# Another order of all steps in a Hedgehog attention and Fourier mixing kernel on one core

## The chip, the core and the metric

The kernel runs on one core of a Trainium2 chip. Its engines are TensorE (PE, with its weight loads shown apart as PEld), VectorE (DVE), ScalarE (ACT), GpSimd (POOL) and SyncE (SP, which here only issues transfers). Each engine executes its own instructions in the order in which the program wrote them, and waits where an operand is not there yet. Transfers are issued by POOL (queue q0) and SP (queue q1) and carried out by 16 DMA engines. The metric is the time of one execution on the device, in microseconds.

## The reference

Eight batches of eight heads with 576 positions and head dimension 64. Linear attention with a feature map of exponentials is followed by a two-dimensional Fourier mix, a normalisation and a feed-forward layer of hidden width 2048:

```python
def phi(x):
    proj = np.einsum('bhsd,df->bhsf', x, w_phi)
    proj = proj - np.max(np.abs(proj), axis=-1, keepdims=True)
    return np.concatenate([np.exp(proj), np.exp(-proj)], axis=-1)
q_p, k_p = (phi(q), phi(k))
kv = np.einsum('bhsf,bhsd->bhfd', k_p, v)
z = np.sum(k_p, axis=2)
num = np.einsum('bhsf,bhfd->bhsd', q_p, kv)
den = np.einsum('bhsf,bhf->bhs', q_p, z)[..., None] + 1e-06
x = (num / den)                      # heads side by side: (8, 576, 512)
X = np.fft.fft(np.fft.fft(x, axis=1), axis=2)
u = x + np.real(X).astype(np.float32)
mu = np.mean(u, axis=-1, keepdims=True)
var = np.mean((u - mu) ** 2, axis=-1, keepdims=True)
un = (u - mu) / np.sqrt(var + 1e-06)
ch = np.maximum(un @ w_ch1, 0.0) @ w_ch2
out = u + ch
```

## The kernel before

The eight batches run through one software pipeline: while PE computes the feed-forward layer of one batch, the attention and the mix of the next are put between its matmuls. Everything is cut into 1238 steps. A step is what a generator issues up to its next yield: a few matmuls on PE and what belongs to them on the other engines. A string PLAN (lines 23 to 37) holds one letter for each step. The kernel walks through it, and each letter calls the next step of its stream; at the end of a batch's steps a stream goes on to the next batch. So PLAN alone sets the order of the instructions on every engine. Nothing else reorders them.

The streams, with the lines that matter:

- F, forward: 16 hidden blocks (matmuls psf, L1224, from the normalised input UT and the first weights W1b; ACT's relu into HT at L1229 and L1231) and the out blocks (pso, L1241, L1267, L1286, from HT and the second weights W2b; DVE adds the residual at L1247, then a store).
- M, mixing: for each head a product of keys and values (kv, L887 and L891; ACT copies it to kvh, L895) and its use by the queries (pn_, L944, L987), then the Fourier mix: pm (L1021), DVE's CEO (L1025, L1034), psD (L1045), ACT's casts to ET and DT (L1050 to L1057), px (L1075), pu (L1104), added to X by DVE (L1089, L1094).
- D, fold: DVE folds X into R (L903 to L927), ACT casts one row to HI (L916, L917), on which pm waits.
- N, normalise: UN (L1139, L1144, L1150) and UT, its transpose, in batch 0 on PE (L1159) and later by a transfer on SP's queue (L1167).
- P, T, R, S: features of keys and queries. The keys' tail of 64 positions is projected at L477 (ps) and its exponentials K4p and K4n are L482 and L483; the main part is projected at L491 (psk) with exponentials KPp and KPn (L497). S scales V by factors from ACT (V4N and V4P at L451, VCn and VCp at L466, with ACT's L447 and L461). In batch 0 that is L852 and L869, with ACT's factors from L862.
- K, V, Q: fetch of the next batches by POOL (L284, into KS, VS, QS); A and B: their transposes by SP (L408 to L422).
- W: two steps. POOL issues the transfer of W1b (L93) and later that of W2b (L95), 2 MB each as they are stored in bf16.
- C and H: constants, and the four sines SS, CS, SD, CD (L238 to L249); POOL's L197 to L218 make their arguments. Z: zeros and ones in padded tiles (L268 to L277). G and J: the first transposes on PE (pst, L368).
- Y: fillers (L1338), four matmuls on ones whose result nobody reads.

Before the first letter, load_first (L336) has SP issue the first batch's K, Q and V, which go into tiles that hold W2b and HT later. V's main part comes in two transfers: heads 0 to 3, then heads 4 to 7. The first batch's heads are taken in pairs, in the order 0, 3, 2, 1, so pair 3 is the first that needs the second half of V.

Of the kernel before, what the change touches and what calls it, by code (L numbers as in the profile page):

```python
# [20 lines left out]


PLAN = (
    "CCZCYYZYGGCTZVTRZKGTGRZWGJTTSJYRSJTQTTPPYTYRPTJMRJTMSMMSPSTKPTPTZMYTMMQTMTPMCQTMMTMTBDMHKMHKHDDHYAHY"
    "DYMYMHYTMMVMRTQMTNMMYTNTQNNYSFNMFNFNRVRFSTTPTFMFRSYUNTFWMURFVFFFFUUMTPMFBSTFMNTUTPNUSMFVPPCTFMFTUPQM"
    "TFMFTFPATVMFFFMMFTFMFKMFFMQFMFRTKFMFFRFPFDFFFFTFFFFTDFFFDRTFFFMFFTTDMFRFFFFSFFMFFFTFMSMFRFTMTTNMTFMN"
    "FPTMMFSSMTPMFTPPMTFFFMFFQNMPTFBSFMFFQMFFPTFFMNNUAMFFMFMFVTRTFFMFFVRVFFKMFKFFFFTMFMFFFFQMFPFDFFTPFRFF"
    "FTFDPFFTFFDDFFRFFTMFFFTMFFMMBSFFMSFRFTMMTFTNNFMFMMMKFTFMTSTFFFFSMPPTMTFFFFFMFSFMFPTMQQVFFFPTKFFMNNNM"
    "FFMFFMFFUMFFMFMFFFAMTRTVFFRTVFFFFFQMFFFDFDFTFFFDRFTPDFFFTPFFRFFTMFFFFTMMMFSFFRSFTMFTFMTTFNFTFMFNSMMM"
    "FMBSFKTTMQNFFFNPFMTFFFMFTPPFMFSFMNFPQMUTFVFKFPAFFMMFMFFVMFFMTFMFFMFFFMRTFRVFFTFFFQMFFFFTDDFRFFFFTFDP"  # L30
    "FFDFTPFFFRFTMTFFFFFMMMFFRFSFSTMSTFFMTFTFFNMFFTNMMMMSTTFMFFQNFTFPMFFFMFVNFMTBPPFSFMFFTPFMKFFFMFFQPNMF"
    "FMAUKFFMFFFMTTFRFRFMFFFTSFFFFVTMFFFRMTQFFFMTFFFFDFDFFFRFDFTFFDMFTFMFFMFSMFMRFTFFTMFTFTFFTMNNFPSMMMMV"
    "TFFSMTPMSTQFFMTPMFTFBQMFPPPFFMFFMFNVFPFFANNUMFFMFMTFMFFMFFMFFRTFRMFFFFFFFVTTPFSFFRFVFFMTFDFFTFFFDFDR"
    "FFFFFTDMTMFFFFFMMFFSFRFTMFTTTMNFMTNMFFFFMSFMMPSTFMFFFNFPTMFFFFFFMTPPSFMFFMFPTFMFFPNFFTMFNMFFMFMFFUFM"
    "FMFFFFMMFFFFFFMFFFFDFFFDFDFFFDFMFFMFFMFFMMFFMNMFFNFFFFFFMFMFMFFFFFFFFFFFFFFFFFFFNFFFFFNFNFFFUFFFFFFF"
    "FFFFFFFFFFFFFFFFFFFFFFFFFFFFFFFFFFFFFF"
)

# [1368 lines left out]
```

## Time and profile before

| | us |
|---|---|
| median of 3 runs | 425.31 |
| lowest and highest | 424.94 and 427.0 |
| span of the profiled execution | 423.1 |
| first hidden matmul of batch 0 (psf) | 53.6 |
| first out matmul of batch 0 (pso) | 85.2 |
| first hidden matmul of batches 2, 3, 4 | 158.2, 205.3, 252.4 |
| end of the last matmul | 418.3 |

The page gives busy time, then the span in forty slices, the DMA queues, the chain of work that ended last, and the costliest groups. The row of the granted TensorE clock (PEclk) has a digit for each slice, 9 being full speed. In a timeline a row gives start and length in us, the engine, the line, what is written from what, and how many instructions are put together (x8); brackets at its end hold the engine's idle time ahead of it and what ended it.

### The profile page before, as it was taken

The page shows a single profiled execution, that of the slowest core. Times are in us where ns is not written, and L with a number is a line of the kernel's source. Part 1 is how long each engine was busy: PE and PEld are TensorE (multiplying, and loading weights), DVE is VectorE, ACT ScalarE, POOL GpSimd, SP SyncE. Part 2 cuts the span into 40 slices and gives each one's busy share as a digit, 9 for nine tenths or more (in the row PEclk, how much of TensorE's full clock was granted, in tenths as well). Part 3 has the DMA queues.
Part 4 walks back from the last instruction along what each step waited for, and adds up shares of the span by engine and source line. Part 5 has one row for each costly group of instructions (what it writes and reads, how often), then busy time and mean ns, then how long its engine had stood idle before and what let it go on. Part 6 is the DMA issues. An engine that isn't in the chain of part 4 may idle for free.

```text
span 423.1 us, 10390 instructions
## 1 busy us (share of the span) xinstructions
PE 397.4 (94%) x4093; PEld 256.1 (61%) x4122; DVE 331.1 (78%) x681; ACT 306.3 (72%) x626; POOL 207.8 (49%) x271
## 2 busy tenths in 40 slices
PE   8787798999899999999999999999999999999995
PEld 3454475744676558655675558665766567656563
DVE  4989788798979976998779885898989786968103
ACT  6978799748975899489847898588868887353460
POOL 7982688525646077706673282834755331500000
PEclk9999999999999999999999999999999999999999
DMA  8999959984569468853899069954895081103313
GB/s 218 206 165 163 148 88 174 145 83 76 89 102 180 72 101 106 123 84 49 112 153 138 2 91 136 131 71 66 117 138 77 14 102 32 27 0 72 72 26 87
DMA packets 108761, 42.70 MB, mean 101 GB/s; under 512 B 82857, under 2 KB 103721, under 8 KB 108713
## 3 DMA queue, kind: packets, MB, share of 16 engines
q0 software_dynamic: 45936, 16.60, 37.1%
q1 hardware_dynamic: 62215, 24.85, 34.8%
q8 instruction: 32, 0.52, 0.5%
q10 hardware_dynamic: 562, 0.59, 0.5%
q14 instruction: 16, 0.13, 0.1%
HBM read 36.77 MB, written 9.44 MB: 109 GB/s over the span
## 4 chain that ended last, share of the span: by engine, by line
PE 61%; DVE 20%; ACT 8%; POOL 5%; DMA 2%; issue 2%; DVEq 0%; ACTq 0%; POOLq 0%
PE psf L1224 21%; PE pso L1241 19%; DVE R L903 3%; PE kv L887 3%; DVE cb L999 3%; DVE tg L994 2%; PE pso L1267 2%; PE psD L1045 2%; DMA UT<-UN 2%; PE pu L1104 2%; PE psq L547 1%; DVE MK L511 1%; PE psk L491 1%; PE psh L597 1%; DVE X L1094 1%
## 5 line engine op out<-in xcount | busy, mean ns | idle before, releaser
L1224 PE MATMUL psf<-UT,W1b 128*128 128x320 bf16 (+1 forms) x1024 | 142.5, 286 | 2.4 <-DMA UT<-UN 1.5
L1241 PE MATMUL pso<-W2b,HT 128*128 128x512 bf16 x467 | 117.1, 379 | 1.7 <-issue 0.5
L1224 PEld LDWEIGHTS <-W1b 128*128 128x128 bf16 x1024 | 94.0, 98 | 29.7 <-issue 4.3
L1229 ACT ACTIVATE HT<-psf 128x320 bf16<-128x320 f32 x128 | 53.5, 442 | 27.0 <-PE psf L1224 21.6
L1241 PEld LDWEIGHTS <-HT 128*128 128x128 bf16 x496 | 44.8, 98 | 44.6 <-issue 2.6
L1002 POOL TENSOR_TENSOR X<-cb,rd 128x320 f32<-128x320 f32 x56 | 41.5, 746 | 38.6 <-DVE rd L1001 37.3
L466 POOL TENSOR_TENSOR VCn<-VS,VCn 128x512 bf16<-128x512 bf16 x28 | 29.7, 1061 | 38.1 <-ACT VCn L461 35.3
L1231 ACT ACTIVATE HT<-psf 128x512 bf16<-128x512 f32 x64 | 37.9, 605 | 12.6 <-PE psf L1224 12.0
L555 DVE TENSOR_REDUCE MQ<-psq 128x8 f32<-128x1024 f32 (+1 forms) x32 | 34.3, 1084 | 13.4 <-PE psq L547 13.2
L1247 DVE SCALAR_TENSOR_TENSOR X<-pso,rs,X 128x512 f32<-128x512 f32 x31 | 22.8, 735 | 21.6 <-PE pso L1241 21.6
L497 ACT ACTIVATE KPn<-psk 128x1024 bf16<-128x1024 f32 x28 | 28.6, 1021 | 14.0 <-DVE MK L511 13.9
L497 ACT ACTIVATE KPp<-psk 128x1024 bf16<-128x1024 f32 x28 | 28.7, 1025 | 11.1 <-PE psk L491 11.1
L451 POOL TENSOR_TENSOR V4N<-VS,V4N 64x256 bf16<-64x256 bf16 x14 | 8.7, 623 | 53.9 <-ACT V4N L447 53.4
L511 DVE TENSOR_REDUCE MK<-psk 128x8 f32<-128x1024 f32 x28 | 33.9, 1212 | 1.0 <-ACT KPp L497 0.7
L1094 DVE TENSOR_TENSOR X<-pu,X 128x512 f32<-128x512 f32 (+3 forms) x49 | 23.3, 526 | 11.2 <-PE pu L1104 8.9
L466 POOL TENSOR_TENSOR VCp<-VS,VCp 128x512 bf16<-128x512 bf16 x28 | 29.7, 1059 | 0.0
L606 ACT ACTIVATE QPHP<-psh 128x1024 bf16<-128x1024 f32 x28 | 28.9, 1031 | 0.8 <-PE psh L597 0.6
L606 ACT ACTIVATE QPHN<-psh 128x1024 bf16<-128x1024 f32 x28 | 29.0, 1035 | 0.0
L1150 ACT ACTIVATE UN<-X,MV 128x512 bf16<-128x512 f32 (+1 forms) x35 | 24.5, 723 | 5.4 <-DVE MV L1175 3.1
L1174 DVE BATCH_NORM_STATS2 st<-X 128x6 f32<-128x512 f32 (+1 forms) x40 | 27.1, 677 | 0.3
L1190 POOL TENSOR_TENSOR rs<-VE,mhalf 128x5 f32<-128x5 f32 (+1 forms) x9 | 10.3, 1145 | 29.0 <-DVE VE L1189 29.0
L987 PEld LDWEIGHTS <-QPHP 128*128 128x128 bf16 x280 | 21.2, 99 | 4.6 <-DVE cb L999 1.0
(465 smaller groups left out, 825.0 us busy)
## 6 DMA issues: line engine op xcount, KB each, us to landing
out_dram<-X SPq DMA_DIRECT2D x15, 256.0 KB
out_dram<-X SPq DMA_DIRECT2D x60, 64.0 KB
QS<-in_q_dram POOLq DMA_DIRECT2D x14, 256.0 KB, 6.2
KS<-in_k_dram POOLq DMA_DIRECT2D x7, 512.0 KB, 7.4
VS<-in_v_dram POOLq DMA_DIRECT2D x14, 256.0 KB, 5.1
W1b<-in_moe_w_ch_dram POOLq DMA_DIRECT2D x1, 2048.0 KB, 13.1
W2b<-in_moe_w_ch_dram POOLq DMA_DIRECT2D x1, 2048.0 KB, 14.8
W2b<-in_k_dram SPq DMA_DIRECT2D x2, 512.0 KB
```

What stands on the lines that cost most here:

```text
L466: nc.gpsimd.tensor_tensor(out=VC[:, hs, :, 0:D], in0=values[b][0][:, hs, :].rearrange("p h (j d) -> p h j d", d=D), in1=VC[:, hs, :, D:D + ...
L497: nc.scalar.activation(out=KP[:, hs, :, :].rearrange("p e (jp jj) f -> p jj (e jp) f", jj=2), in_=psk[:], func=AT.Exp, scale=sgn,)
L511: nc.vector.tensor_reduce(out=MK[:, 2 * pr:2 * pr + 2, :].rearrange("p e (jp jj) -> p jj (e jp)", jj=2), in_=tiles[pr][:], axis=AX.X, op=A ...
L555: nc.vector.tensor_reduce(out=o, in_=i[:], axis=AX.X, op=ALU.max, apply_absolute_value=True)
L606: nc.scalar.activation(out=o, in_=psh[:], func=AT.Exp, scale=sgn)
L1002: nc.gpsimd.tensor_tensor(out=X[:, :, D * h:D * h + D], in0=cb[:, :, 0:D], in1=rd[:].to_broadcast([128, 5, D]), op=ALU.mult,)
L1094: nc.vector.tensor_tensor(out=to, in0=more, in1=to, op=ALU.add)
L1174: nc.vector.bn_stats(out=st[0:M, :], in_=X[0:M, c, 0:C])
L1224: nc.tensor.matmul(ps, lhsT=W1b[:, cc, 128 * hh:128 * hh + 128], rhs=UT[:, cc, lo:hi], start=(cc == 0), stop=(cc == NCC - 1),)
L1229: nc.scalar.activation(out=HT[:, hh, lo:hi], in_=ps, func=AT.Relu, scale=-1.0)
L1231: nc.scalar.activation(out=HT[:, hh - 1:hh + 1, lo:hi], in_=psw[:].rearrange("p (a n) -> p a n", a=2), func=AT.Relu, scale=-1.0,)
L1241: nc.tensor.matmul(po[:], lhsT=HT[:, hh, at:at + 128], rhs=W2b[:, hh, :], start=(hh == 0), stop=(hh == NHH - 1),)
```

## The change

Only the string PLAN is replaced. The number of steps and of each letter are the same; all fourteen lines of it differ. Its first line before and after:

```diff
 PLAN = (
-    "CCZCYYZYGGCTZVTRZKGTGRZWGJTTSJYRSJTQTTPPYTYRPTJMRJTMSMMSPSTKPTPTZMYTMMQTMTPMCQTMMTMTBDMHKMHKHDDHYAHY"
+    "ZYZCYYCCGCGTWGRTGZTTJZYRPYTSJTJRSPTGJSTRPTKJTMMYMRSSTMPKTPTQPTBMTMZQMMTTPMCQZMMTTMVDTHHYMHAMYDHDDYYY"
```

POOL in the first 17 us, before the change. QPHP, QPHN, V4P, V4N and HI are padded tiles that are filled once; gs, gc and ga are arguments of the sines; VS and KS are parts of batch 1's values and keys:

```order
L197 TENSOR_SCALAR gs<-ga,pn 128x320 x3
L268 MEMSET QPHP 128x8x64
L268 MEMSET QPHN 128x8x64
L212 TENSOR_SCALAR gc<-gc,pn 128x512
L215 TENSOR_SCALAR gc<-gc 128x512
L218 TENSOR_TENSOR ga<-ga,gc 128x512
L271 MEMSET V4P 128x520
L284 DMA VS_249<-in_v_dram 64x4x64 x2
L271 MEMSET V4N 128x520
L284 DMA KS_265<-in_k_dram 64x8x64
L274 MEMSET HI_105 128x512
L93 DMA W1b<-in_moe_w_ch_dram 128x4x2048
```

(between the last two there is a second memset of the same kind, for HI's other tile). POOL at the same place in the changed program:

```order
L268 MEMSET QPHP 128x8x64
L268 MEMSET QPHN 128x8x64
L197 TENSOR_SCALAR gs<-ga,pn 128x320 x3
L212 TENSOR_SCALAR gc<-gc,pn 128x512
L215 TENSOR_SCALAR gc<-gc 128x512
L218 TENSOR_TENSOR ga<-ga,gc 128x512
L93 DMA W1b<-in_moe_w_ch_dram 128x4x2048
L271 MEMSET V4P 128x520
L271 MEMSET V4N 128x520
L852 TENSOR_TENSOR V4N<-HT,V4N 64x4x64 x2
L852 TENSOR_TENSOR V4P<-HT,V4P 64x4x64 x2
L869 TENSOR_TENSOR VCn<-HT,VCn 128x8x64
```

W1b's transfer moved ahead of the V4 memsets; the transfers of VS and KS and the HI memsets moved behind the scaling of the first V; the two L268 memsets moved ahead of L197.

ACT around the fold of batch 0, before the change (HI is the row that pm waits for; ps and psk are projected keys of batch 1, ET and DT results of the mix):

```order
L247 ACTIVATE SD<-ga 128x512
L916 CAST HI_105<-R 1x257
L917 CAST HI_105<-R 1x255
L249 ACTIVATE CD<-ga,halfpi 128x512
L482 ACT_TABLE_LOAD
L482 ACTIVATE K4p<-ps_880 128x512
L483 ACTIVATE K4n<-ps_880 128x512
L1053 CAST ET<-psD 128x289
L1054 CAST ET<-psD 128x289
L1057 ACTIVATE ET<-psD 128x2x31
```

And in the changed program:

```order
L247 ACTIVATE SD<-ga 128x512
L249 ACTIVATE CD<-ga,halfpi 128x512
L916 CAST HI_105<-R 1x257
L917 CAST HI_105<-R 1x255
L482 ACT_TABLE_LOAD
L482 ACTIVATE K4p<-ps_861 128x512
L483 ACTIVATE K4n<-ps_861 128x512
L497 ACTIVATE KPp<-psk 128x2x4x128
L497 ACTIVATE KPn<-psk 128x2x4x128
L1053 CAST ET<-psD 128x289
L1054 CAST ET<-psD 128x289
L1057 ACTIVATE ET<-psD 128x2x31
```

The last sine (CD) moved ahead of the HI casts, and the first exponentials of KPp and KPn of batch 1 ahead of the ET casts. On PE the projection for K4p (L477) stands directly ahead of pm (L1021) in the changed program, and behind pm and eight fillers before; the projection for that first KPp (L491) stands between pm and the first psD (L1045), and before the change behind all of psD and px.

Behind the first out matmul the letters of all streams are dealt anew as well. On PE, runs of matmuls of the same shape are longer there: 136 changes between array shapes (which rows and columns of the array a matmul uses) in place of 151.

More of the change, by code (lines that the diff above doesn't have):

```diff
@@ L23 @@
 PLAN = (
-    "CCZCYYZYGGCTZVTRZKGTGRZWGJTTSJYRSJTQTTPPYTYRPTJMRJTMSMMSPSTKPTPTZMYTMMQTMTPMCQTMMTMTBDMHKMHKHDDHYAHY"
[L25 to L33, printed above, removed]
@@ L34 @@
-    "FFFFFTDMTMFFFFFMMFFSFRFTMFTTTMNFMTNMFFFFMSFMMPSTFMFFFNFPTMFFFFFFMTPPSFMFFMFPTFMFFPNFFTMFNMFFMFMFFUFM"
-    "FMFFFFMMFFFFFFMFFFFDFFFDFDFFFDFMFFMFFMFFMMFFMNMFFNFFFFFFMFMFMFFFFFFFFFFFFFFFFFFFNFFFFFNFNFFFUFFFFFFF"
+    "ZYZCYYCCGCGTWGRTGZTTJZYRPYTSJTJRSPTGJSTRPTKJTMMYMRSSTMPKTPTQPTBMTMZQMMTTPMCQZMMTTMVDTHHYMHAMYDHDDYYY"
+    "HTMTMTMHRYVMRSMQTVKTQPMNMYTYNRNTMTSNUNYTFMMFRFNFNUFFSFMKNRUFMFNPSFWMTTPMFCFFTNBFFPFUMPTFSMTFMPTFMTUF"
+    "TUPQTFMUFFATMFMFMFFMFMFMFMKFTRFFRFTFFFFFDDQDTVPQFVFFDVTFFFMTFTFFMFFRRFFFFSVFFKSFMMFTFFFFTSMRFFSMTMTN"
@@ new lines @@
+    "FFNPMMBTFMMTPSFPMTMTPMFTFFMTPFMFFQFMFPFTFFMNNNMFMFFVMFMFFMVFFMFMFATTFRURFTMKFFFFFFFTTPFFDFFFRDFFQKFF"
+    "FPTQFFFDFFRFDFTMFFFTTSFMMMFFFFRBFMSFPTMFTNFSSFMNMFFFMMMTTTFFVFPFFSMTPMTFFFMQFFNMFNFFMPTFAMFFPTFMNMFV"
+    "FMFFMMUFFMFFMFFFMFFTMFFFDTRTTFFQKFFRDFFVFTFFFDRPFFFDSFFTPFFRFFMFFFTQTTFFMMFFFSMRFMFTSTTMFFFNTFMFNMMM"
+    "FFMTTMFFFNKPMSTNSPFMFFFTNPQMFFFFUMFBVTFPMFFMFPMMVFFFMAFMFFFTTMFRFSFTMFFFFMFRFDKFFTFFTFMQFRFFFFFDFSDK"
+    "PPFDSFFTFFFFRTMFFFTVFTMFFMMQFRFFPSMFTTTMMSNFNFMMFFMMFFBPFMTTFFFFMVQTPMFVFMFTFMFNFFMPTFKMTFAFFFPFMFTN"
@@ L36 @@
+    "TFMFNUFFTFRMFFRFFMFFFSFFFMFFMFFFMTFFFDTMRFDFFFTFFFQFDVDFFFQFRMFTTMTFFFMSMFRFFMFTTTQMFKMFMTNNSMFMFMFT"
+    "SPFFMFFTPMFFTMTPMTFFFNMPSBFFFPPFVMFFMFFAPNNMUFFMMFFFMFFMFFMFTTFFRMFFFFTSRFFFTPTFFFMFRFFDDFFTFFFFRFFF"
+    "DDFVFTVTMFFMFTFFMFFMFRSFMFTTSTMMFFNNFTMSFMNMMFFFFTPFFFMTPMFPTSFFMNFFFMFFPPMFFMFTPTFFFMNFUMFFMFMFFMFF"
+    "MFFFMMFFFMFFFFFDFFDFFFFDFFDFFMFFFFMMMFFMFFFMFNFFMNFFFMNFMFFFNFMFFFFFFFFFFFFFFNFFFFUFFFFFFFFFFFFFFFFF"
     "FFFFFFFFFFFFFFFFFFFFFFFFFFFFFFFFFFFFFF"
```

## Prediction

> **What bounds the kernel now.** I read the page first, for which engine is full and at what clock, then the windows of the stages, then the chain of waits and the timelines of the stages that are not full.
>
> ```profile
> span 423.1 us, 10390 instructions
> PE 397.4 (94%) x4093; PEld 256.1 (61%) x4122; DVE 331.1 (78%) x681; ACT 306.3 (72%) x626; POOL 207.8 (49%) x271
> PEclk9999999999999999999999999999999999999999
> 0.00:45.90 45.90, 36.31 (x423) 21.35 (x423) 37.53 (x83) 35.01 (x64) 33.88 (x60) 1.00 1.06 184
> 45.90:78.00 32.10, 27.44 (x347) 19.64 (x347) 24.12 (x61) 31.02 (x67) 22.60 (x28) 1.00 1.09 142
> 78.00:418.30 340.30, 333.64 (x3326) 215.06 (x3354) 268.98 (x538) 240.31 (x496) 151.29 (x184) 1.00 0.66 86
> L1224 PE MATMUL psf<-UT,W1b 128*128 128x320 bf16 (+1 forms) x1024 | 142.5, 286 | 2.4 <-DMA UT<-UN 1.5
> ```
>
> A window's row gives start, end and length, then busy time on PE, weight loads, DVE, ACT and POOL, the granted clock and the DMA share. From 78 on PE is busy 333.64 of 340.30 us: that stage only becomes shorter if PE has less to do or waits less for UT. Of the first 45.9 us PE is busy 36.31, part of it fillers, so others set that pace; from 45.9 to 78 ACT does (31.02 of 32.10). What the head gains or loses is passed on whole, since PE's backlog behind it is full. The profiled span is 423.1 us and the median of the three runs 425.31: what lies around the span is 2.2 us, which I add to every sum.
>
> **The head: the weight load.** POOL is in the chain of waits here.
>
> ```profile
> 8.86 2.52 SPq L336 DMA_DIRECT2D HT<-in_v_dram  x4
> 10.44 1.27 POOL L218 TENSOR_TENSOR ga<-ga,gc 128x512 f32<-128x512 f32 x1
> 14.78 1.01 POOL L274 MEMSET HI<- 128x512 bf16 x2
> 15.71 0.79 POOL L93 DMA_DIRECT2D W1b<-in_moe_w_ch_dram  x1
> 19.31 1.06 POOL L869 TENSOR_TENSOR VCn<-HT,VCn 128x512 bf16<-128x512 f32 x1
> 23.30 1.06 POOL L869 TENSOR_TENSOR VCp<-HT,VCp 128x512 bf16<-128x512 f32 x1
> 25.76 1.06 POOL L869 TENSOR_TENSOR VCn<-HT,VCn 128x512 bf16<-128x512 f32 x1 [1.40 <-ACT VCn L862]
> ```
>
> W1b is issued at 15.71, and the chain runs over POOL's scaling of V (L852, L869) until about 24.4, where pair 3 is done. In the new order W1b stands directly behind L218. Two V4 memsets, the VS and KS transfers and the HI memsets no longer come before it, so it is issued at about 11.7 (L218's end) instead, 4.0 us earlier. The transfers of V, which SP issued up to 11.4, are then still running. What that does is read from the queues.
>
> ```profile
> q1 hardware_dynamic: 553, 0.55, 107.8%
> ...
> q1 hardware_dynamic: 241, 0.23, 33.5%
> ...
> q0 software_dynamic: 193, 0.79, 97.1%
> q1 hardware_dynamic: 192, 0.05, 9.3%
> ...
> W1b<-in_moe_w_ch_dram POOLq DMA_DIRECT2D x1, 2048.0 KB, 13.1
> ```
>
> The first row is 13.0 to 14.5: V alone in SP's queue q1, 553 packets of 1 KB, 369 a us, 23 a us on each of the 16 DMA engines. The second is 14.5 to 16.5: the last 241, which at that pace are through at about 15.2. The third and fourth are 22 to 26, where W1b in POOL's queue q0 meets transposes in q1: 193 packets against 192. The engines alternate one for one, and a packet of W1b (4 KB) costs 16 x 4.0 x 0.971 / 193 = 0.322 us. W1b has 2 MB / 4 KB = 512 packets, 32 an engine, together 10.3 us.
>
> Its first packet comes some 1.5 us after the issue (13.1 from issue to landing, less 10.3, with part of the rest at the end): about 13.2. V then has about 241 + 553 x 1.3/1.5 = 720 packets left, 45 an engine. That is more than 32, so all of W1b passes in between and V ends 10.3 us later, at 25.5; with 1.0 for the landing 26.5. The two scalings of pair 3 (the second half of V) end 2 x 1.06 later, at 28.6, where they ended at 24.4. Behind that point the new order is faster: the 1.40 us that POOL waits for L862 (which stands on ACT behind kvh evictions) falls by some 0.85, as three evictions are ahead of it and not four. So the fold starts **3.4 us later**. Bounds: V through before W1b's first packet, -2.5 (two transfer issues and three memsets no longer stand before L852); a first packet with all of V still to go, +4.5.
>
> Row 193:192 first: the Trainium skill, "DMA: Bandwidth & Descriptors", section "Queues, rings and completion order", says that an engine goes round the queues in whole packets of about 9 to 17 descriptors each. If V's groups held 16 rows and W1b's 8, an estimate by that page, 45 rows of V would let only three groups, 24 rows of W1b, 7.7 us, pass; V would land at 23.9 and the sum below be 2.6 us lower, 422.3. The trace shows equal numbers, so I keep one for one; no run here shows these two transfers together.
>
> **The clock.** PE has nothing else ready while it waits for pair 3: what stands before it in the new order is what before ended at 23.1 (and a projection, 0.4), so about 5 us idle.
>
> ```profile
> 22.94 0.19 PE L891 MATMUL kv<-V4N,K4n 128*128 128x65 bf16 x1
> 24.42 0.29 PE L887 MATMUL kv<-VCp,KPp 128*128 128x65 bf16 x4 [1.28 <-POOL VCp L869]
> ...
> 418.30:422.50 4.20, 0.00 (x0) 0.00 (x0) 0.48 (x1) 0.00 (x0) 0.00 (x0) 1.00 0.26 74
> 422.60:423.10 0.50, 0.00 (x0) 0.00 (x0) 0.00 (x0) 0.00 (x0) 0.00 (x0) 0.50 0.00 0
> ...
> 1.11 5.45 PE L1338 MATMUL idle<-ones_b 128*128 128x512 bf16 x12 [1.11 <-DVE keep L130]
> 36.73 3.18 PE L1338 MATMUL idle<-ones_b 128*128 128x512 bf16 x12
> ```
>
> After the last matmul the clock stays 1.00 for 4.2 us and then is 0.50. Twelve fillers at the start took 5.45 us, at full clock 3.18: one spell of half clock costs 2.3. An idle time of 5 us passes 4.2 by less than it is uncertain, so I take 0.4 of that, **+0.9**; bounds 0 and 2.3, or more in a rival below. The Trainium skill, "TensorE: Matmul & The Clock Gate", section "Part 1: The HAM clock gate", gives a free-running window of 3.4 us, one idle window halving the clock; 5 us would hold a whole one in about (5 - 3.4)/3.4, half of the cases, an estimate that gives +1.1 in place of 0.9. The trace's 4.2 lies between one window and two, so it agrees.
>
> **After the fold.** ACT waits twice.
>
> ```profile
> 40.96 0.41 ACT L916 CAST HI<-R 1x257 bf16<-1x257 f32 x1 [1.44 <-DVE R L912]
> 41.58 0.72 ACT L249 ACTIVATE CD<-ga,halfpi 128x512 bf16<-128x512 f32 x1
> 44.59 1.28 ACT L482 ACT_TABLE_LOAD   x1 [2.29 <-PE ps L477]
> 46.85 0.41 ACT L1053 CAST ET<-psD 128x289 bf16<-128x289 f32 x1
> 41.94 2.10 PE L1338 MATMUL idle<-ones_b 128*128 128x512 bf16 x8
> 44.10 0.41 PE L477 MATMUL ps<-wphi,KT 64*64 64x128 bf16 x8
> ```
>
> The table load for L482 waits 2.29 us for keys that stand on PE behind pm and eight fillers. In the new order they are projected before pm, and the last sine (CD) runs ahead of HI, in the 1.44 us wait. So 2.29 + 0.72 = 3.0 us leave ACT's path, and ACT has two key exponentials done before ET. DVE's CEO still comes at its old distance from the fold, which I put at 0.5: **-2.5**, bounds 0 and -3.0. As ACT is the bound to 78, this is passed on.
>
> **Steady state.** Counted from the new order, PE changes between its array shapes 136 times after the first out matmul, and 151 times before the change.
>
> ```profile
> 92.18 1.46 PE L1241 MATMUL pso<-W2b,HT 128*128 128x512 bf16 x6
> 93.47 0.38 PE L1021 MATMUL pm<-HI,ones_b 128*128 128x512 bf16 x1
> 93.90 0.81 PE L1241 MATMUL pso<-W2b,HT 128*128 128x512 bf16 x3
> 94.65 0.40 PE L491 MATMUL psk<-wphi,KT 64*128 64x128 bf16 x8
> ```
>
> Six pso of one shape take 93.47 - 92.18 = 1.29, 0.215 each; three from 93.90 would end at 94.55, and the 64-row psk starts at 94.65. A change costs 0.10, so fifteen fewer give **-1.5** (bounds 0 and -3.0). The eight more changes ahead of it (62 for 54) lie where PE is not the bound.
>
> ```profile
> 205.29 1.47 PE L1224 MATMUL psf<-UT,W1b 128*128 128x256 bf16 x12 [1.00 <-DMA UT<-UN]
> 252.41 1.48 PE L1224 MATMUL psf<-UT,W1b 128*128 128x256 bf16 x12 [0.47 <-DMA UT<-UN]
> ```
>
> PE waits for UT 1.00 us at batch 3 and 0.47 at batch 4. Between mixing's last step and the first hidden matmul the new order has 8.00 and 7.82 us of PE work, for 7.59 and 7.49: **-0.7**, bounds 0 and -1.5. Other moved steps (keys, queries, fetches) fill the same PE time with the same rows; their rings of PSUM buffers are about as tight, so I put them at 0, with 1.5 to both sides. W2b's load goes out three steps of F later; its landing after 14.8 us still leaves 3 us to the first out matmul.
>
> **Sum.** 3.4 - 2.5 + 0.9 - 1.5 - 0.7 = -0.4: a span of 422.7, a time of **424.9 us**, no change that can be measured. A measurement here can tell about 0.5%, 2.1 us, from none.
>
> **Rivals.**
> 1. V is through before W1b comes (the software queue starts later than 1.5 us; POOL's two L268 memsets now stand ahead of L197, and may push L218). Then 3.4 becomes -2.5 and the clock costs nothing: 424.9 - 5.9 - 0.9 = 418.1. For it: a small transfer that POOL issued at 12 into the full queues took 3.9 us, most of it waiting. Against it: even that comes before V is through. 0.2.
>
> ```profile
> VS<-in_v_dram POOLq DMA_DIRECT2D x2, 32.0 KB, 3.9
> ```
>
> 2. Slower: the wait for pair 3 passes the gate by a wide margin, and the clock stays half until the fold, because the work of the heads comes in small pieces with waits between. From 28.37 to 34.69 the chain is nearly all PE, 6.3 us, which at half clock is 6.3 more and not 0.9: 430.3. It decides from 4.2 us idle on. For it: an idle time of 5. Against it: that passes 4.2 by less than the error of the landing time, and steps of several heads lie ready behind pair 3.
>
> ```profile
> 28.37 0.86 PE idle L1338 x4
> ...
> 34.36 0.33 PE pn__730 L944 x10
> ```
>
> 0.2.
> 3. The order does not keep its steady gain: new waits for PSUM buffers (keys for the next batch stand closer to M's steps) take 1.5 and the 2.2 of both steady terms do not come: 424.9 + 3.7 = 428.6. For it: 6.7 us of PE idle from 78 on are few, so any new wait shows. 0.15.
>
> **How the numbers follow.** Forecast 0.45, rival 1 0.2, rival 2 0.2, rival 3 0.15. Half a per cent puts the bounds at 423.2 and 427.4. The forecast's own range is 422 to 428, by the bounds of its terms: 0.3 of it within, 0.1 below (the middle price of the steady terms is not their greatest), 0.05 above. Rival 1 is faster, rival 2 slower; of rival 3 0.1 stays within, where only part of the gain is lost, and 0.05 is slower. So faster 0.1 + 0.2 = 0.3, same 0.3 + 0.1 = 0.4, slower 0.05 + 0.2 + 0.05 = 0.3. The range, 418.0 to 429.8, leaves out half of rival 1 and half of rival 2, 0.2 in all.
>
> **What would show it.** W1b issued near 11.7 and pair 3's VCp ending near 28.6 (right), or by 23 (rival 1); PEclk below 1.00 in windows from 28 to 36 (rival 2); ACT's table load at L482 with no wait; the first psf of batches 3 and 4 with waits under 0.7 us; PE idle from the first out matmul on falling by about 2 us. I am wrong if the fold starts earlier than before, or if the stage behind 85 us changes by more than 4.

## The result, and the profile after

The changed kernel takes 433.0 us, median of four runs (432.95, 433.1, 431.56 and 441.57), the kernel before 425.1. The ratio is 1.016, 95% interval 1.0128 to 1.0192: **slower by 1.6%**, where I had forecast 424.9 and a range up to 429.8. The run of 441.57 lies 2% above the others and is left out of the ratio, as such runs are from the ratios below.

The page of the changed kernel, the same lines as before the change:

```profile
span 431.1 us, 10416 instructions
PE 405.1 (94%) x4122; PEld 258.1 (60%) x4122; DVE 332.6 (77%) x681; ACT 307.3 (71%) x626; POOL 207.9 (48%) x271
PEclk9899999999999999999899998999999999999999
L1224 PE MATMUL psf<-UT,W1b 128*128 128x320 bf16 (+1 forms) x1024 | 144.4, 289 | 7.8 <-DMA UT<-UN 7.3
```

PE looks as busy as before (94%), but that share hides the loss: the clock row now has an 8 in three slices, and the wait of the first layer for UT rose from 1.5 to 7.3 us. (Of PE's larger busy time, 7.7 us, about half is a matter of records: 29 pso are missing in the trace of before and none here, and pso's busy time is 121.0 us for 117.1.)

Where the 8 us arise is seen from windows cut at the same events in both traces: the first HI cast, the first hidden matmul of batch 0, the first out matmul, then the first hidden matmul of batches 2, 3, 4 and 5 (the table goes on to the end of the last matmul). First the changed kernel:

```profile
0.00:38.80 38.80, 34.68 (x404) 20.50 (x404) 30.66 (x73) 32.21 (x61) 30.83 (x57) 0.96 1.03 189
38.80:52.20 13.40, 10.10 (x98) 5.38 (x98) 12.96 (x31) 12.49 (x25) 7.90 (x12) 1.00 0.89 123
52.20:80.80 28.60, 27.62 (x367) 20.76 (x366) 23.10 (x59) 25.60 (x57) 18.65 (x21) 1.00 1.07 132
80.80:154.20 73.40, 71.32 (x695) 42.32 (x693) 65.31 (x125) 55.40 (x111) 43.94 (x55) 1.00 0.94 119
154.20:205.10 50.90, 46.67 (x498) 29.88 (x495) 43.51 (x85) 39.03 (x81) 26.08 (x32) 1.00 0.70 90
205.10:258.90 53.80, 48.73 (x498) 30.63 (x498) 41.83 (x75) 35.44 (x72) 28.51 (x36) 0.97 0.74 93
258.90:308.20 49.30, 48.16 (x494) 31.28 (x494) 37.48 (x75) 38.63 (x79) 24.15 (x29) 0.97 0.62 89
```

And two of the same stages before the change:

```profile
158.20:205.30 47.10, 45.38 (x469) 29.29 (x474) 40.18 (x82) 38.36 (x79) 26.02 (x32) 1.00 0.66 90
205.30:252.40 47.10, 46.14 (x486) 30.10 (x490) 38.19 (x77) 35.74 (x74) 27.00 (x34) 1.00 0.92 101
```

| stage | before | after | difference |
|---|---|---|---|
| start to the first HI cast | 41.0 | 38.8 | -2.2 |
| to the first hidden matmul | 12.6 | 13.4 | +0.8 |
| to the first out matmul | 31.6 | 28.6 | -3.0 |
| to batch 2 | 73.0 | 73.4 | +0.4 |
| batch 2 to batch 3 | 47.1 | 50.9 | +3.8 |
| batch 3 to batch 4 | 47.1 | 53.8 | +6.7 |
| batch 4 to batch 5 | 48.1 | 49.3 | +1.2 |
| batch 5 to the last matmul | 117.8 | 118.1 | +0.3 |

So the head, where I expected the fold to be late, is 4.4 us faster up to the first out matmul, and three stages in the middle lose 11.7. PE's waits there, from the timeline of the changed kernel:

```profile
205.05 2.49 PE L1224 MATMUL psf<-UT,W1b 128*128 128x256 bf16 x12 [3.81 <-DMA UT<-UN]
242.11 1.01 PE L1045 MATMUL psD<-SS,CEO 128*128 128x289 bf16 x6 [1.65 <-ACT HT L1229]
258.93 1.05 PE L1224 MATMUL psf<-UT,W1b 128*128 128x256 bf16 x8 [2.58 <-DMA UT<-UN]
```

Two of them are followed by half clock, in windows laid over it:

```profile
205.40:208.70 3.30, 3.30 (x26) 1.94 (x24) 0.15 (x1) 1.17 (x2) 0.98 (x2) 0.50 0.47 58
259.95:263.30 3.35, 3.35 (x33) 2.67 (x30) 0.00 (x0) 2.77 (x6) 0.41 (x1) 0.50 0.71 134
```

Each such spell is 3.4 us at half speed and costs PE 1.7 us of work. In the stage from batch 3 to 4 there are one spell (1.7), the wait at psD (1.65, and 0.42 at the next one) and 2.1 us more for UT: 5.9 of the 6.7. The bracket at psD names ACT's HT. ACT was late there itself, held by DVE's L511 (from ACT's timeline):

```profile
240.72 1.02 ACT L497 ACTIVATE KPn<-psk 128x1024 bf16<-128x1024 f32 x1 [3.13 <-DVE MK L511]
```

That L511, at 239.47, stands on DVE behind the fold, which the second place below explains.

Two places explain the waits. **The first is a fetch in the way of the transposes.** POOL's issue ahead of batch 3's first hidden matmul in the changed kernel, from its timeline:

```profile
194.25 0.93 POOL L284 DMA_DIRECT2D KS<-in_k_dram  x1
```

SP's, from the same:

```profile
196.92 2.67 SPq L1167 DMA_TRANSPOSE UT<-UN  x2
```

The DMA queues of the changed kernel for 3.6 us from that issue on (packets, MB, share of 16 engines):

```profile
q0 software_dynamic: 981, 0.49, 107.8%
q1 hardware_dynamic: 323, 0.23, 20.8%
```

The queues of the kernel before, for 3.6 us from its own UT issue at 199.9 on (a K transpose that SP issued at 202.57 is among them):

```profile
q1 hardware_dynamic: 1136, 0.37, 78.9%
```

Both kernels store the same rows of X ahead of UT and transpose the same UT. Now 981 packets of batch 5's K fetch fill the engines, and q1 (stores, then UT) moves 323 packets in 3.6 us where it moved 1136. The small packets of the transposes begin 3.3 us after the issue of UT (at 200.2) and not 1.2 us (at 201.1). One for one, as the prediction read it off W1b, does not describe these two queues: 981 stand against 323, and why is open. In the chain of the changed kernel the piece "UT<-UN" is 6.62 us long:

```profile
198.29 6.62 DMA UT<-UN
```

Before the change it was 3.90:

```profile
201.25 3.90 DMA UT<-UN
```

**The second is DVE behind POOL.** Batch 4's fold in the changed kernel, from DVE's timeline:

```profile
235.26 4.02 DVE L920 TENSOR_TENSOR R<-R 128x510 f32<-128x510 f32 x2
```

POOL's at the same time:

```profile
235.09 0.94 POOL L284 DMA_DIRECT2D KS<-in_k_dram  x1
236.04 1.07 POOL L466 TENSOR_TENSOR VCn<-VS,VCn 128x512 bf16<-128x512 bf16 x1
237.06 1.06 POOL L466 TENSOR_TENSOR VCp<-VS,VCp 128x512 bf16<-128x512 bf16 x1
```

The same DVE line before the change:

```profile
232.71 1.27 DVE L920 TENSOR_TENSOR R<-R 128x510 f32<-128x510 f32 x2
```

Two L920 take 1.27 us together before the change and 4.02 here; the first of them is 3.4 us long, and ends 0.6 us behind POOL's second L466, about the length that it needs by itself (0.68). In the order of before POOL had nothing to do at that place. This is so far a coincidence in time; x3_scale_later below tests it.

### The profile page after: what moved, and what is told of

It reads as the page before. It is cut to its first block, busy times and chain, and to the rows that moved or that the text cites. A ratio compares the mean times of both kernels' runs of the same rounds, so it can differ in the third digit from the quotient of the medians.

```text
span 431.1 us, 10416 instructions
## 1 busy us (share of the span) xinstructions
PE 405.1 (94%) x4122; PEld 258.1 (60%) x4122; DVE 332.6 (77%) x681; ACT 307.3 (71%) x626; POOL 207.9 (48%) x271
## 4 chain that ended last, share of the span: by engine, by line
PE 52%; DVE 23%; ACT 16%; DMA 4%; issue 3%; POOL 1%; DVEq 0%; ACTq 0%; POOLq 0%
PE psf L1224 20%; PE pso L1241 14%; DMA UT<-UN 4%; DVE cb L999 4%; DVE tg L994 3%; DVE X L1094 3%; PE kv L887 2%; PE psD L1045 2%; ACT QPHN L606 2%; PE pso L1267 2%; DVE MK L511 2%; ACT QPHP L606 2%; DVE st L1174 2%; DVE R L920 1%; ACT KPp L497 1%
## 5 line engine op out<-in xcount | busy, mean ns | idle before, releaser
L1224 PE MATMUL psf<-UT,W1b 128*128 128x320 bf16 (+1 forms) x1024 | 144.4, 289 | 7.8 <-DMA UT<-UN 7.3
L1241 PE MATMUL pso<-W2b,HT 128*128 128x512 bf16 x496 | 121.0, 379 | 0.0
L1224 PEld LDWEIGHTS <-W1b 128*128 128x128 bf16 x1024 | 95.9, 99 | 36.9 <-issue 6.8
L466 POOL TENSOR_TENSOR VCn<-VS,VCn 128x512 bf16<-128x512 bf16 x28 | 29.6, 1057 | 43.4 <-ACT VCn L461 34.6
L511 DVE TENSOR_REDUCE MK<-psk 128x8 f32<-128x1024 f32 x28 | 33.8, 1209 | 0.0
L497 ACT ACTIVATE KPp<-psk 128x1024 bf16<-128x1024 f32 x28 | 28.6, 1021 | 5.6 <-PE psk L491 5.5
L466 POOL TENSOR_TENSOR VCp<-VS,VCp 128x512 bf16<-128x512 bf16 x28 | 29.5, 1055 | 0.0
L284 POOL DMA_DIRECT2D QS<-in_q_dram x28 | 23.4, 836 | 1.1 <-DMA QT<-QS 1.1
```

What stands on the lines that cost most here:

```text
L466: nc.gpsimd.tensor_tensor(out=VC[:, hs, :, 0:D], in0=values[b][0][:, hs, :].rearrange("p h (j d) -> p h j d", d=D), in1=VC[:, hs, :, D:D + ...
L497: nc.scalar.activation(out=KP[:, hs, :, :].rearrange("p e (jp jj) f -> p jj (e jp) f", jj=2), in_=psk[:], func=AT.Exp, scale=sgn,)
L511: nc.vector.tensor_reduce(out=MK[:, 2 * pr:2 * pr + 2, :].rearrange("p e (jp jj) -> p jj (e jp)", jj=2), in_=tiles[pr][:], axis=AX.X, op=A ...
L1224: nc.tensor.matmul(ps, lhsT=W1b[:, cc, 128 * hh:128 * hh + 128], rhs=UT[:, cc, lo:hi], start=(cc == 0), stop=(cc == NCC - 1),)
L1241: nc.tensor.matmul(po[:], lhsT=HT[:, hh, at:at + 128], rhs=W2b[:, hh, :], start=(hh == 0), stop=(hh == NHH - 1),)
```

## Experiments

All kernels differ from one of the two only in PLAN. A step is written as letter, batch and number (K5.1 is the second K fetch of batch 5).

### Head against rest

The first two exchange the parts at step 320, about the first hidden matmul of batch 1.

```diff
 h1_new_head
-PLAN before
+first 320 steps of PLAN after, then all others in the order of PLAN before
 h2_new_rest
-PLAN after
+first 320 steps of PLAN before, then all others in the order of PLAN after
```

> The first 320 steps of the new order (up to the first hidden matmuls of batch 1), then all that is left in the order of before. In the trace of the change the head is 4.4 us shorter at the first out matmul (80.8 for 85.2) and 4.1 us at the first hidden matmul of batch 2 (154.2 for 158.2); everything is lost between there and 260 us. If head and rest are independent: 425.1 - 4.2 = 420.9 us, between 420 and 422. If the early head merely moves a wait (the steady part is bound by something that does not start earlier, such as transfers), the gain melts away: 424 to 426.

Measured: 420.8 us, ratio to before 0.986 (0.9819 to 0.9897). First out matmul at 81.2, and the stages behind it as before the change (47.1 us from batch 2 to batch 3).

> The mirror of it: the first 320 steps as before, then what is left in the new order. If the loss belongs to the new order of the steady part alone: 433.0 + 4.2 = 437.2 us, 435 to 439. If the loss comes from transfers that arrive at an unlucky moment because the head is early, it goes with the old head: 425 to 429.

Measured: 438.7, ratio 1.029 (1.0259 to 1.0322), with a UT wait of 4.03 at batch 3. Head and rest add up: the head brings 5.3 to 5.7 us (426.2, the kernel before in that comparison, less 420.8; 438.7 less 433.0), the rest of the new order costs some 12. The new head on the old rest beats both kernels.

### The fetch

```diff
 x1_k5_early (PLAN after)
-K5.0 F2.30 ... F2.66 N3.2 K5.1 P4.2
+K5.0 K5.1 F2.30 ... F2.66 N3.2 P4.2
```

> The changed kernel with one step moved: the second K fetch of batch 5 (512 KB, issued by POOL at 194.3 us, three us ahead of batch 3's UT transposes) stands directly behind the first K fetch of that batch, some 30 us earlier. Theory A (the fetch's packets in q0 slow the stores and the UT transposes in q1, so that UT lands late and PE idles 3.8 us at 205.05, after which the clock is 0.66 for 5 us): the wait at batch 3 falls to under 1.2 us, the clock there stays 1.00, and the time falls by 3.8 - 0.5 + 1.7 = 5.0 to about 428 (427 to 429.5). Theory B (UT is late because its inputs are late: the order of the mixing steps, DVE and ACT): the fetch does not matter, 432 to 434, with the wait at batch 3 still over 3 us.

Measured: 428.5 (ratio to before 1.0037, 1.0006 to 1.0068), 4.5 less than the change by the medians of two comparisons, in which the kernel before took 425.1 and 426.2; by the ratios it is 5.2. The wait and the slow clock at batch 3 are gone, as PE's timeline shows; psD and UT of batch 4 wait as they did (1.65 and 2.40):

```profile
204.06 1.47 PE L1224 MATMUL psf<-UT,W1b 128*128 128x256 bf16 x12 [0.34 <-DMA UT<-UN]
```

The window behind it has full clock:

```profile
205.00:210.00 5.00, 5.00 (x77) 3.98 (x75) 3.35 (x7) 4.74 (x11) 5.00 (x7) 1.00 0.92 146
```

The mirror of it puts the collision into the kernel before:

```diff
 b1_k5_late (PLAN before)
-T3.17 K5.1 F2.11 ... R4.4 S4.1 F2.55
+T3.17 F2.11 ... R4.4 S4.1 K5.1 F2.55
```

> The kernel of before with one step moved: the second K fetch of batch 5 (512 KB) goes from some 30 us before the UT transposes of batch 3 to 2 to 3 us before them (between two scalings of V on POOL, at about 197.5), the place that the change gave it. Theory A: the wait for UT at batch 3, 1.0 us before, grows to 3.5 to 4.5 and the clock falls to 0.5 for a window of 3.4 us behind it: 425.5 + 3 + 1.7 = 430 (428.5 to 431). Theory B (the fetch is harmless, the new order of the other steps makes UT late): 425 to 426.5.

Measured: 429.3, ratio 1.0088 (1.0065 to 1.0111). One fetch moved costs 3.8 us (429.3 less 425.5, the kernel before in that comparison). The wait in PE's timeline:

```profile
206.77 2.51 PE L1224 MATMUL psf<-UT,W1b 128*128 128x256 bf16 x11 [2.73 <-DMA UT<-UN]
```

Slow clock follows here too, in the window:

```profile
205.00:210.00 5.00, 3.23 (x24) 2.51 (x25) 1.12 (x2) 1.04 (x2) 2.36 (x3) 0.66 0.75 145
```

The next kernel was to clear the transposes of batches 4 and 5 as well.

```diff
 x2_all_fetches (as x1_k5_early, and)
-F3.61 F3.62 B6.0 ... M5.2 V6.0 Q6.2 ... F4.0 V6.1 F4.1
+F4.4 B6.0 ... F4.5 V6.0 Q6.2 ... F4.7 V6.1
-K7.0 ... Q7.2 M5.21 F4.57 K7.1
+K7.0 K7.1 ... F5.1 Q7.2
```

> The same, and the transfers around the UT transposes of batches 4 and 5 moved as well: batch 6's K transposes and its V and last Q fetches behind batch 4's first hidden matmuls, batch 7's second K fetch directly behind its first, its last Q fetch behind batch 5's first hidden matmuls. Theory A: the UT waits at batch 4 (2.6) and batch 5 (0.9) and the slow clock behind them (1.7 each) go as well, except for what a late fold leaves at batch 4 (one DVE instruction of L920 takes 3.4 us there in place of 0.7): 433 - 5 - 1.1 - 3.4 = 423.5, between 421 and 426. Theory B: 432 to 434. If L920's long instruction is a chance of that one execution, batch 4's wait goes entirely and the time is at the lower end.

Measured: 427.2 (ratio 1.0015, 0.9986 to 1.0044), a miss by 3 to 4 us. Batch 5's wait (0.92 in the changed kernel) is gone, but batch 4's has grown to 4.2, and PE's clock is 0.50 from 255 to 260. POOL's timeline tells why the edit did nothing there: the V fetches that I had put behind batch 4's first hidden matmuls were issued as early as ever, from 245.03 to 248.55.

```profile
245.03 1.28 POOL L284 DMA_DIRECT2D VS<-in_v_dram  x2
```

And PE's wait:

```profile
255.74 0.61 PE L1224 MATMUL psf<-UT,W1b 128*128 128x256 bf16 x2 [4.20 <-DMA UT<-UN]
```

A place in the program is a time only on an engine that is kept waiting there. POOL had no instruction with a wait between the old place and the new one, so it ran ahead.

### POOL beside DVE's fold

```diff
 x3_scale_later (as x1_k5_early, and)
-F3.39 S5.1 D4.2 K6.1 P5.0 P5.1 F3.40 D4.3 S5.2 ... R5.3 T5.6 M4.16
+F3.39 D4.2 K6.1 P5.0 P5.1 F3.40 D4.3 ... R5.3 T5.6 M4.16 S5.1 S5.2
```

> The changed kernel with batch 5's second K fetch early (as in x1_k5_early) and one thing more: the first two scalings of batch 5's V (POOL L466, four instructions, with ACT's factors) stand behind the first psD step of batch 4's mix and no longer on both sides of batch 4's fold (DVE L920). In five traces of the new order that one L920 takes 3.41 us in place of 0.68, from 235.26 to 238.68, while POOL issues a K fetch and runs L466 twice up to 238.12; in the order of before, where POOL waits at that place, it takes 0.68. Theory A (POOL's work holds DVE's access up until it pauses): L920 back to 0.7 us, the wait at psD (1.65) gone, UT 2.7 us earlier, the wait at batch 4 (2.4) down to about 1.3 and the slow clock behind it (1.7) gone: 428.5 - 1.65 - 1.1 - 1.7 = 424 (423 to 426). Theory B (L920 is slow there for another reason, its operands or PSUM): L920 stays at 3.4 us and the time within 1 us of 428.5.

Measured: 424.7 (ratio 0.9982, 0.9956 to 1.0008). L920 is back to 1.27 for two, batch 4's wait for UT down to 0.46, and no half clock follows. But POOL's L466 now runs beside the next DVE steps, CEO (L1034, L1070), and these become long instead, so that psD still waits 1.71. DVE's timeline of x3_scale_later:

```profile
230.31 1.27 DVE L920 TENSOR_TENSOR R<-R 128x510 f32<-128x510 f32 x2
235.47 2.02 DVE L1034 TENSOR_TENSOR CEO<-R 128x381 bf16<-128x381 f32 x2
237.41 1.02 DVE L1070 CAST CEO<-R 128x6 bf16<-128x6 f32 x1
```

POOL's L466 is longer there too: 1.36, from 235.71, for 1.06 elsewhere. PE's wait:

```profile
239.60 0.91 PE L1045 MATMUL psD<-CS,CEO 128*128 128x289 bf16 x6 [1.71 <-DVE MK L511]
```

Elsewhere two L1034 take 1.03 us, L1070 0.17. The total came out as expected, its parts did not: the wait for UT fell by 1.9 (2.40 to 0.46) where I had put 1.1, and the waits at psD by 0.4 (1.65 and 0.42 to 1.71) where I had put 1.65.

That POOL's work holds L920 is shown by this run, but not which part of it: the K fetch's issue, K6.1, went out earlier as well, at 226.69, since POOL had nothing to wait for ahead of it. Another fetch's issue speaks for the scalings: in the changed kernel POOL issues QS from 230.72 to 231.65, and DVE's L903 beside it (from 230.99), which also has two inputs in SBUF, takes its usual 1.28 for two.

```diff
 x4_v6_later (as x3_scale_later, and)
-M5.2 V6.0 Q6.2 ... F4.0 V6.1 F4.1 ... F4.7 K7.0
+M5.2 Q6.2 ... F4.0 F4.1 ... F4.7 K7.0 V6.0 V6.1
```

> As x3_scale_later, with the two V fetch steps of batch 6 (VS, POOL issues at about 245 to 249, beside the UT transposes of batch 4) put behind the K fetch step that follows, which waits on POOL until the K transposes are through, at about 258; so they really go out later. (In x2_all_fetches the same steps were moved on paper only: nothing that waits stood between, and POOL issued them at 245.0 to 248.6 all the same.) If fetches that run beside them slow the UT transposes, the wait at batch 4 falls to under 0.5 us and the time to 1 us below x3: 422 to 424. If not, the time is that of x3.

Measured: 426.2 (423.07 to 431.99; ratio 1.0012, 0.998 to 1.0043). The fetches do go out later, at 261.7, but the time does not fall: nothing is shown on these two, and in the profiled execution V's second half came late in the head, as the next part tells.

### W1b and the first loads

My forecast rested on W1b meeting V. In the changed kernel it hardly did: POOL issued W1b at 11.16, but the queue has none of its packets up to 15. The queues from 13 to 15:

```profile
q1 hardware_dynamic: 714, 0.71, 104.7%
```

And from 15 to 16:

```profile
q0 software_dynamic: 32, 0.13, 65.1%
q1 hardware_dynamic: 210, 0.20, 57.4%
```

So 4 us pass from issue to first packet, not 1.5, and V is nearly through. To see whether the alternation itself is real, W1b was issued at 3.1:

```diff
 w1_first (PLAN after)
-Z0.0 Y0.0 Z0.1 ... T0.0 W0.0 G0.2
+W0.0 Z0.0 Y0.0 Z0.1 ... T0.0 G0.2
```

> The changed kernel with the W1b step first of all, so that POOL issues the 2 MB ahead of its L268 memsets, at about 4 us in place of 11.2, while SP's K, Q and V loads are all in the queue. My forecast said that W1b's packets alternate with V's one for one from 1.5 us after the issue; in the trace of the change W1b was issued at 11.16 but its first packet came at about 15.2, when V was nearly through, and V was not late. If packets alternate as soon as the descriptors are there: W1b's first packets at 6 to 8 us, V lands some 8 us later, at about 24, and the time rises by 5 to 8, to 438 to 441. If a transfer of POOL's gets going only when the other queue is nearly empty: first packet still at 14 to 15, time 432 to 434.

Measured: 444.0, ratio 1.042 (1.0367 to 1.0467). W1b's first packets come from 7.4 on, 4.3 us after the issue, while q1 is full, so they do not wait until the other queue has emptied. The queues from 7 to 8:

```profile
q1 hardware_dynamic: 503, 0.28, 104.1%
q0 software_dynamic: 9, 0.04, 18.1%
```

From 12 to 16 us the queues go one for one:

```profile
q0 software_dynamic: 189, 0.77, 95.1%
q1 hardware_dynamic: 189, 0.10, 11.7%
```

And POOL waits ten microseconds for V, in its timeline:

```profile
22.88 1.31 POOL L852 TENSOR_TENSOR V4N<-HT,V4N 64x256 bf16<-64x256 f32 x2 [10.01 <-DMA HT<-in_v_dram]
```

That W1b takes turns with the first loads and makes V late is as I had it, with a price above my estimate (11 us for 5 to 8); the moment was wrong, by some 2.5 us. In the profiled execution of x4_v6_later, whose head is the changed kernel's, V's second half is late. POOL's timeline there:

```profile
25.39 1.06 POOL L869 TENSOR_TENSOR VCn<-HT,VCn 128x512 bf16<-128x512 f32 x1 [6.11 <-DMA HT<-in_v_dram]
```

And its queues from 18 to 24 us:

```profile
q0 software_dynamic: 304, 1.25, 102.8%
q1 hardware_dynamic: 40, 0.04, 2.4%
```

V's last packets pass at 6.7 a us where V alone makes 357. One engine that alternates with W1b (0.33 us a packet) passes 3 a us, so it is what two or three of the sixteen engines would make, on which W1b would have begun too soon; that is an estimate, no view shows the engines one by one. The first out matmul comes at 88.4, 7.6 us later than in the changed kernel's own profile. A kernel with W1b safely behind V:

```diff
 h3_w_later (as h1_new_head, and)
-T0.0 W0.0 G0.2 ... P0.0 Y0.4 T0.4 S0.0 J0.1
+T0.0 G0.2 ... P0.0 Y0.4 T0.4 S0.0 W0.0 J0.1
```

> As h1_new_head (new head, old rest), with W1b's issue moved behind the scaling of V's tail (POOL L852), to about 17 us, where V's 2 MB are through on every DMA engine. In one trace of the new head (x4_v6_later) some engines began W1b before V's last packets, V's second half came at 25.4 in place of before 19, and the first out matmul was 7.3 us later; in the five other traces it did not happen. If that is the cause of the scatter upwards of kernels with the new head (441.6 once among 432 to 433, 436.4 once among 425 to 431): median as h1, 420 to 422 (W1b lands at 30 and is first used at 52), and no execution more than 2 us above it. If the scatter has another cause, it stays.

Measured: 421.7 (420.83 to 422.36), ratio 0.9898 (0.9879 to 0.9918). W1b is issued at 16.98 and the time is that of h1_new_head within its interval: W1b's early issue is not what makes the new head fast. Six runs lie within 1.6 us; that the scatter of the others comes from W1b alone is likely, not shown.

### Where the head's gain comes from

Three kernels take parts of the new head into the kernel before.

```diff
 b2_fold_part (PLAN before)
-H0.2 D0.1 D0.2 H0.3 Y0.7 A1.0 H0.4 Y0.8 D0.3 Y0.9 M0.14 Y0.10 M0.15 H0.5 Y0.11 T1.0 M0.16 ... T1.1
+H0.2 A1.0 Y0.7 D0.1 H0.3 D0.2 D0.3 Y0.8 Y0.9 Y0.10 H0.4 T1.0 M0.14 T1.1 M0.15 M0.16 H0.5 ...
 b3_pool_part (PLAN before)
-V1.0 ... K1.0 ... Z0.4 W0.0 ... S0.0 ... K1.1
+S0.0 W0.0 ... K1.0 K1.1 V1.0 Z0.4
 b4_pool_and_fold: both
```

> The kernel of before, with only the 23 steps around batch 0's fold in the order that the change gave them (keys for K4 ahead of pm, the last sine ahead of HI, the first KPp ahead of ET). My forecast's term for this part was -2.5 us, bounds 0 and -3.0. If it is right and passed on whole: 425.3 - 2.5 = 422.8 (422 to 423.5). If the gain at the fold is taken back before the first out matmul (ACT stays full to 78 us and does the same work), 425.

Measured: 425.6, ratio 0.9995 (0.9979 to 1.0011). ACT's wait ahead of the table load is gone, but ACT now waits for psD instead, in its timeline:

```profile
41.69 1.28 ACT L482 ACT_TABLE_LOAD   x1
47.47 0.40 ACT L1050 CAST DT<-psD 128x289 bf16<-128x289 f32 x1 [1.76 <-PE psD L1045]
```

The first out matmul, at 84.9, is 0.3 us earlier than before the change.

> The kernel of before, with only the head of POOL's order changed: the first VS and KS transfers, the HI memsets and W1b's issue stand behind the scaling of V's tail (L852) or of all of V (L869) and no longer ahead. In the trace of the change L852 starts at 14.33 in place of 16.51 and the first HI cast at 38.77 in place of 40.96. If this is where the head's first half comes from: HI at about 38.8 and the time 425.5 - 2.2 = 423.3 (422.7 to 424). If the gain is lost again before the first out matmul: 425 to 426.

Measured: 425.3, ratio 1.0003 (0.9984 to 1.0022). POOL's L852 starts at 14.65, 1.9 us earlier, but the first HI cast only 0.24 earlier, at 40.72: POOL's first L869 is 1.0 earlier and not 1.9, since W1b is issued in between, it waits the same 1.40 us for ACT's factors of L862, and DVE's conversion L220, which took 0.42, now runs beside POOL's HI memset (L274) and takes 1.55.

> The same, with the 23 steps around the fold in the new order as well, as in b2_fold_part (which alone took nothing off: 425.6). If POOL's part alone carries: 423.3. If the two together make the head's whole 4.4 us: 421. If the head's second half comes from the order of the steps between the fold and the first out matmul: the time of b3_pool_part.

Measured: 425.9, ratio 1.0006 (0.9989 to 1.0024). Neither part, nor the two together, makes the new head. Its gain lies in other steps of the 320 or in their interplay; which, stays open.

### The price of a shape change

```diff
 s1_more_changes (as h1_new_head; ten times in batches 1 to 5, of this kind)
-F2.7 P3.5 T3.16
+P3.5 F2.7 T3.16
```

> As h1_new_head, with ten steps of features (T and P, 64-row matmuls) put one place further from steps of their own shape, between two F steps: 231 changes of the array shape in place of 211, all of them after 85 us, with the same work. At my 0.093 to 0.10 a change: 420.8 + 1.9 = 422.7 (422 to 423.5). If a change costs nothing where PE is full: 420.8 (420 to 421.5).

Measured: 422.6, ratio 0.9918 (0.9897 to 0.994). From the first out matmul to the last matmul, s1_more_changes:

```profile
80.20:415.10 334.90, 330.00 (x3258) 210.04 (x3255) 262.69 (x520) 235.66 (x486) 150.46 (x183) 1.00 0.64 88
```

And h3_w_later, which runs the same steps there:

```profile
82.10:415.10 333.00, 328.28 (x3258) 210.38 (x3255) 262.67 (x520) 235.46 (x486) 150.43 (x182) 1.00 0.64 89
```

20 changes more, 1.9 us more: 0.095 each, the price that I took. The trace of h1_new_head, which runs the same steps as h3_w_later there, takes 333.8 us (81.16 to 414.96), by which it would be 0.055. The intervals of the whole times overlap, so the price rests on these traces and is rough.

## Why the prediction was wrong, point by point

- **V held up by W1b, +3.4: wrong sign.** The step that failed is "Its first packet comes some 1.5 us after the issue". It came 4 us after; V was nearly through, and the fold began 2.2 us earlier. That was rival 1, which I had at 0.2. The lone row for it (a small transfer of 3.9 us) was the better guide than W1b's own start in a queue that had emptied. One for one and 0.322 us a packet held (w1_first). The 0.85 that I took off for L862 did not come in the profiled execution: POOL waits 1.51 us for it, 1.40 before; in h1_new_head, with the same head and full clock there, it waits 0.87.
- **After the fold, -2.5: not shown as a step of its own.** The wait for L482 went as I said, but the stage from HI to the first hidden matmul became 0.8 longer, and b2_fold_part gained nothing. "As ACT is the bound to 78, this is passed on" was too quick: what ACT may do earlier only counts where DVE's CEO and PE's psD do not hold it two casts later. The new head gains 3.0 us between the first hidden and the first out matmul.
- **The clock, +0.9: the place was wrong.** There is one spell of half clock in the head too, from 17.6 to 21.0, and the fold is early all the same; the two behind the UT waits cost 1.7 each. I had it follow an idle time of over 4.2 us; it followed waits of 3.8 and 2.6.
- **Shape changes, -1.5: about right in price.** 0.055 to 0.095 against 0.10; fifteen fewer are worth 0.8 to 1.4 us, which the waits bury.
- **UT waits, -0.7: wrong sign, +5.8** (7.3 for 1.5). I compared how much work PE has to cover the wait, and took the wait's other side, 3.9 us from UN to UT, as given. It became 6.6.
- **"Other moved steps (keys, queries, fetches) fill the same PE time with the same rows ... so I put them at 0, with 1.5 to both sides": this is where the forecast broke.** They are free for PE. They are not free for the 16 DMA engines and for DVE: K5.1 alone costs 3.8 (b1) to 4.5 (x1; 5.2 by the ratios), S5.1 and S5.2 beside the fold 3.8 (x3 against x1; 2.3 by the ratios). Together they are 8.3 (7.6 by the ratios) of the 12 us that the new rest loses; the rest of the loss is not explained.
- **Rival 3** (the steady gain lost to new waits, 428.6) had the right place and side, but the wrong waits and a third of the price. Rival 2 did not happen.

## What to carry to other kernels

When an order changes, follow the queues as closely as the busy engine: ask of each transfer that is waited for what else will be under way in its time, and of each POOL instruction which DVE instruction runs beside it. A step placed later in the program goes out later only if its engine is kept waiting there. And a wait on a full PE can be paid twice: waits of 2.4 to 4.2 us were followed by half clock in these traces, waits of up to 1.7 were not. A fetch and two scalings in the wrong place undid a better head.

## What the runs showed of the hardware

- Half clock came in whole pieces of 3.4 us, on one grid: it began at 17.59, 205.32 and 259.93 in the changed kernel. The last two lie 54.61 us apart, 16 pieces of 3.413, the first two 187.73, 55.0 of these. In the piece ahead of each PE was busy 1.87, 0.25 and 0.96 us; another piece, busy 1.76, was followed by full clock (the last row):

```profile
14.20:17.59 3.39, 1.87 (x29) 1.50 (x28) 3.10 (x6) 3.27 (x10) 2.85 (x5) 1.00 1.12 289
201.90:205.30 3.40, 0.25 (x3) 0.26 (x4) 2.18 (x5) 0.87 (x2) 3.40 (x4) 1.00 0.96 156
256.50:259.90 3.40, 0.96 (x11) 0.88 (x12) 2.05 (x4) 0.43 (x2) 0.24 (x1) 1.00 1.14 212
239.45:242.86 3.41, 1.76 (x11) 0.73 (x10) 3.38 (x7) 2.14 (x4) 0.31 (x1) 1.00 1.53 186
```

  The Trainium skill, "TensorE: Matmul & The Clock Gate", section "Part 1: The HAM clock gate", says that the window is free-running and 3.4 us long; the trace agrees. That a window in which PE is busy for 28% can be followed by half clock is measured here; the first and the last row show that the busy time alone does not decide.
- DVE's L920 (two inputs in SBUF) took 3.4 us for 0.68, so it was held for 2.7 us across a fetch's issue and two POOL instructions, in each of the five traces that have these steps side by side. The Trainium skill, "SBUF — State Buffer", section "SBUF: two separate sides", says that such a DVE instruction and a POOL instruction that reads SBUF lock each other out for the length of an instruction. The trace agrees that DVE is blocked, but for longer than one instruction: it was not let in between POOL's two. In x3_scale_later both sides became longer instead (L1034 1.0 for 0.5, L466 1.36 for 1.06).
- W1b, POOL's 2 MB, had its first packet 1.4 to 1.7 us after the issue where SP's queue had emptied (kernel before, h3_w_later), and 4.1 to 4.3 us after it beside a full one (changed kernel, w1_first). In h3_w_later, as in the latter two, W1b is POOL's first transfer, so being first is not the reason.
